# The last 1024 tokens of a first mixture as two tiles of 512, with three sets of inputs

## The chip, the cores and the metric

The program runs on one core of a Trainium2 chip. The metric is the device time of one execution in microseconds (us), lower is better; several executions are timed, and the median is given. The engines are named as in the profile: PE is the tensor engine's matmul stream and PEld its weight loads, DVE the vector engine, ACT the scalar engine, POOL GpSimd, SP the engine that issues the DMAs here.

## The reference, cut to what matters

All arrays are float32; the batch is 4, with 8 heads, 576 positions and 64 features.

```python
def attn(q, k, v):                       # (4, 8, 576, 64) each
    # pooled: means over 4 neighbours, full softmax attention over 144 positions, repeated 4 times
    out_up = np.repeat(softmax_attn(pool4(q), pool4(k), pool4(v)), 4, axis=2)
    # local: softmax over |i - j| < 4 only
    out_local = banded_softmax(q @ k.T / 8) @ v
    return out_up + out_local

x = attn(q, k, v).transpose(0, 2, 1, 3).reshape(2304, 512)
h = x @ w_in                             # (512, 2048)
x = (h * np.cos(h)) @ w_out              # first mixture
xn = x / np.sqrt(np.mean(x * x, -1, keepdims=True) + 1e-6) * rms_g
g = xn @ w_gate                          # (512, 1536)
out = (g / (1 + np.exp(-g)) * (xn @ w_val)) @ w_out2     # second mixture
```

## The kernel before

**Tokens and tiles.** The 2304 tokens are nine tiles of 256 (`TT`). A batch of the attention has 576 rows, so it covers two tiles and a quarter. Each tile's attention output is split into a high and a low part (`XH`, `XLO`, the tiles `xh` and `xl`), and every product of a mixture is three matmuls: weight high by x high, weight high by x low, weight low by x high. The weights arrive as 64-bit words and are turned into high and low parts on the chip (`w_conv`, L275: a shift on DVE at L287, an ACT step at L291, a merge on DVE at L293, ACT at L295, a subtraction on POOL or DVE at L298). A converted piece occupies one place of 4 KB a partition and stays; a raw piece occupies one for a time. There are 34 places (`NS`), and 8 more (`NX`) once the attention's memory is closed.

**First mixture.** 72 units, eight to a tile (`unit`, L917, and `second`, L976). A unit computes two 128-column chunks of h for 256 tokens, 24 matmuls 256 wide at L935 into one PSUM bank; then kk, t, sin and t again (L951 to L958) on ACT and DVE, and g split into gh and gl (L969, L971). `second` does 24 more matmuls, 256 wide, at L997, which add up in two banks y over the eight units of the tile. `y_out` (L1005) copies the two banks out on ACT (L1011) and stores them to DRAM (`ysc`). `SEQ` mixes the units of tiles 0 and 1; from tile 2 on they follow one another.

**Inputs of a tile.** There are two sets of x (`xt`). A tile's set is released when its last h product is done (L940), and only then can the attention write the tile after next. `block` (L589) is one local attention block of up to 116 rows: transposes (L603), scores (L640, L646), softmax on DVE and ACT, transposes (L680), values (L705), the sum with the pooled output (L715), and xh on ACT and xl on POOL (L727, L729), which wait for the set. Two tokens `blk` bound how many blocks of batches 1 to 3 are under way. `pooled` (L479) is the pooled attention of a head pair; a block waits for its batch's four (`od`).

**Banks.** PSUM has eight banks. During tiles 0 and 1 four are for y, two for h (`hb`), two for the attention (`att`); after tile 0 both h and the attention get one more.

**Second mixture.** `second_mixture` (L1024) starts when the last tile's x is complete and the last first-mixture weight is converted: it closes the attention's memory, adds `NX` places, and loads and converts 36 pieces. These also need the places of first-mixture weights, which are given back as the last tile uses them (L937 to L938, L999 to L1000). `prep` (L1053) loads a tile's y, normalizes it and writes xh and xl (L1095, L1097). `out_unit` (L1121) and `out_second` (L1181) then do 12 chunks for tile 0 alone, 256 wide, and for four pairs of tiles, 512 wide (L1144, L1201).

**Order.** `Order` writes out the instruction order of all engines ahead of time. Each part (a unit, a block, a conversion) is a generator that yields an engine with an assumed duration, waits for an event or takes a token; the part that can start first goes next, and among nearly equal ones the one with the earlier due time (`DU`, `due`). The assumed durations shape only the order; on the chip, semaphores decide.

Of the kernel before, what the change touches and what calls it, by code (L numbers as in the profile page):

```python
# [25 lines left out]
NX = 42 - NS  # L26
# [3 lines left out]
NQK, NV = 4, 3  # L30
# [14 lines left out]
DU = {"conv": 20, "pool": -260, "blk": -150}  # L45


class Order:
# [65 lines left out]
    def start(self, p):  # L114
# [60 lines left out]
def fused_kernel(ctx: ExitStack, tc, q, k, v, w_in, w_out, w_gate, w_val, w_out2, rms_g, mask, bmask, out):  # L175
# [18 lines left out]
    for n, c in (("t", 2), ("kk", 2), ("g", 2), ("xt", 2), ("n1", 2), ("sq", 1), ("raw", NRAW), ("cv", NCV),  # L194
                 ("blk", 2), ("blk0", 2), ("b2", 5), ("rq", NQK), ("vb", NV), ("od", 2), ("E", 2), ("qs", NQS), ("vh", 2)):
        S_.pool(n, range(c))
# [111 lines left out]
    XH, XLO = (xr.tile([128, 2, 4, TT], F32R, tag=n, name=n) for n in ("xh", "xl"))  # L308
# [81 lines left out]
    def pq_load(b, parts):  # L390
        for w, c, x, m in parts:
            p = yield take("pq")
            t = ap.tile([128, 576], F32, tag=p, name="pq")[:, :512].rearrange("p (u r d) -> p u r d", u=2, r=4)
# [38 lines left out]
    EP = [ap.tile([72, 2, 3, 2, 64], F32, tag=f"E{x}", name="E") for x in range(2)]  # L432
# [13 lines left out]
    def pv(b, hp, t=None, place=None, vh=None):  # L446
# [4 lines left out]
        else:  # L451
# [3 lines left out]
            for _ in range(2):  # L455
                x = yield take("pq")
                p.append(x)
            t = (ap.tile([128, 576], F32, tag=p[0], name="v4")[:, :512].rearrange("p (c x) -> p c x", c=2),
                 ap.tile([128, 576], F32, tag=p[1], name="v4")[:, :256])
# [129 lines left out]
    def block(b, u, raw, pools):  # L589
# [5 lines left out]
        yield take(tok)  # L595
        T = []
# [51 lines left out]
        for x, _ in T:  # L648
            give("b2", x)
        t0 = (S_.cur["t"], "PE")  # L650
# [136 lines left out]
    def start():  # L787
# [3 lines left out]
        for n in [("pq", w, c) for c in range(3) for w in range(2)] + [("qs", w) for w in range(2)] + [("E", hp) for hp in (2, 3)] \  # L791
# [17 lines left out]
        E = EP + [early(("E", hp), [72, 2, 3, 2, 64]) for hp in (2, 3)]  # L809
# [3 lines left out]
        for hp in range(2):  # L813
            yield take("E")
# [57 lines left out]
        S_.add(after(("od", 0), "E", 0, 1), 0.0)  # L872
        S_.add(after(("od", 0), "pq", "pq1"), 0.0)
        S_.add(after(("od", 0), "place", pl["E", 2], pl["E", 3]), 0.0)
# [27 lines left out]
    G = {}  # L902

    def moe():
# [10 lines left out]
        + [(t, u) for t in range(2, NTILE) for u in range(8)]  # L915

    def unit(n):  # L917
        t, u = SEQ[n]
        yield wait(("x", t))
        xh, xl, xi = X[t]  # L920
        for ci in range(2):
            yield wait(("w", 1, 2 * (2 * u + ci)))
# [4 lines left out]
        h3 = bank_tile(i, [128, 2, TT], "h")  # L927
        for ci in range(2):
            wh, wl = W[1, 2 * (2 * u + ci)]
            yield "PE", 1.44  # L930
# [10 lines left out]
        h = h3.rearrange("p c t -> p (c t)")  # L941
# [23 lines left out]
        gh = tp.tile([128, 2, TT], F32R, tag=f"gh{g_i}", name="gh")  # L965
        gl = tp.tile([128, 2, TT], F32R, tag=f"gl{g_i}", name="gl")
        tv = t.rearrange("p (c t) -> p c t", c=2)
        yield "ACT", 0.62
        ACT.activation(out=gh, in_=tv, func=ACTF.Copy)  # L969
        _, e = yield [("POOL", 1.5), ("DVE", 0.8, None, None, GLB)]  # L970
        (POOL if e == "POOL" else DVE).tensor_tensor(out=gl, in0=tv, in1=gh, op=ALU.subtract)  # L971
# [4 lines left out]
    def second():  # L976
        y, yi = {}, {}
        for n in range(8 * NTILE):
            t, u = SEQ[n]
            S_.due(T0 + U1 * n + DS)  # L980
            yield wait(("g", n))
            for ci in range(2):
                yield wait(("w", 1, 2 * (2 * u + ci) + 1))
            if u == 0:
                yi[t] = []
                for _ in range(2):
# [292 lines left out]
```

## Time and profile before

| | us |
|---|---|
| median of 3 executions | 1057.72 (1054.84 to 1058.4) |
| the profiled execution | 1062.11 |
| its span, first to last instruction | 1060.3 |
| PE busy in the span | 1019.4 (96%) |
| DVE / ACT / POOL busy | 518.6 / 491.0 / 252.8 |
| mean granted TensorE clock | 0.982 of full speed |

The span and the rows below are of the profiled execution, which took 4.4 us more than the median. A busy share of a long stretch hides stages with different limits, so the stages are read one by one.

### The profile page before, as it was taken

Reading aid. Unit: us, or ns where it says so; the run is one execution under the profiler, and the core shown is the slowest. Engines: PE = TensorE matmul, PEld = TensorE weight load, DVE = VectorE, ACT = ScalarE, POOL = GpSimd, SP = SyncE. Lnnn points to the kernel's source line nnn. Section 1 sums busy time; section 2 is a strip of 40 time slices with the busy share of each in tenths; the row PEclk is TensorE's granted clock in tenths of the full one; section 3 lists DMA queues with packets and bytes.
Section 4 is the critical chain, followed back from the end, with each engine's and each line's share of the span. In section 5 each row is a group of like instructions: output and inputs, shape, how many; then the busy total and the mean of one; then the engine's idle time right before and its main releaser. Section 6 shows DMA issues by size and latency. Waiting matters only on the chain.

```text
span 1060.3 us, 18859 instructions
## 1 busy us (share of the span) xinstructions
PE 1019.4 (96%) x7736; PEld 927.9 (88%) x7736; DVE 518.6 (49%) x866; ACT 491.0 (46%) x897; POOL 252.8 (24%) x303
## 2 busy tenths in 40 slices
PE   7888889999999999999999988999999999999998
PEld 7788789999999999999999976888888888888886
DVE  3688964655564545344488887312341153112112
ACT  4656785675675445363567865311331142122111
POOL 3857674345441000000044443000000000000000
PEclk9889989999999999999999999999999999999999
DMA  8769532443331111100436550100200020001001
GB/s 237 204 179 280 178 90 77 115 120 95 98 79 29 46 33 49 38 22 2 160 115 224 168 190 2 39 1 1 70 11 1 1 80 1 0 1 40 1 1 40
DMA packets 108134, 82.57 MB, mean 78 GB/s; under 512 B 67344, under 2 KB 95120, under 8 KB 108048
## 3 DMA queue, kind: packets, MB, share of 16 engines
q1 hardware_dynamic: 108048, 81.36, 25.9%
q8 instruction: 61, 1.00, 0.4%
q14 instruction: 25, 0.20, 0.1%
HBM read 71.90 MB, written 9.44 MB: 77 GB/s over the span
## 4 chain that ended last, share of the span: by engine, by line
PE 84%; DVE 8%; ACT 3%; issue 2%; DMA 1%; SPq 1%; POOL 0%; ACTq 0%; DVEq 0%; POOLq 0%
PE gvp L1144 25%; PE y L997 18%; PE h L935 17%; PE o L1201 13%; DVE raww L293 2%; PE bav L705 2%; PE btr L603 2%; PE warm L226 1%; DVE raww L287 1%; PE avp L553 1%; PE bs L646 1%; PE bat L680 1%; ACT E L509 1%; DMA raww<-in_moe_w_in 1%; PE sps L498 1%
## 5 line engine op out<-in xcount | busy, mean ns | idle before, releaser
L1144 PE MATMUL gvp<-xh,ww 128*128 128x512 f32 (+1 forms) x840 | 245.1, 370 | 0.0
L935 PE MATMUL h<-xh,ww 128*128 128x256 f32 x1152 | 225.6, 289 | 4.0 <-DVE t L958 4.0
L997 PE MATMUL y<-gh,ww 128*128 128x256 f32 x1152 | 225.1, 289 | 0.6 <-ACT gh L969 0.6
L935 PEld LDWEIGHTS h<-xh,ww 128*128 128x128 f32 x1152 | 186.7, 194 | 5.9 <-DVE t L958 2.9
L997 PEld LDWEIGHTS y<-gh,ww 128*128 128x128 f32 x1152 | 185.5, 193 | 2.8 <-ACT gh L969 1.1
L1144 PEld LDWEIGHTS gvp<-xh,ww 128*128 128x128 f32 x840 | 154.0, 190 | 26.4
L997 PE MATMUL y<-gl,ww 128*128 128x256 f32 x576 | 164.2, 285 | 4.1 <-DVE gl L971 4.1
L935 PE MATMUL h<-xl,ww 128*128 128x256 f32 x576 | 164.2, 285 | 0.0
L1164 DVE TENSOR_TENSOR sil<-gvp,sil 128x512 f32<-128x512 f32 (+1 forms) x60 | 38.2, 637 | 257.3 <-PE gvp L1144 249.4
L1144 PE MATMUL gvp<-xl,ww 128*128 128x512 f32 (+1 forms) x420 | 155.2, 370 | 0.0
L997 PEld LDWEIGHTS y<-gl,ww 128*128 128x128 f32 x576 | 111.0, 193 | 5.1 <-DVE gl L971 5.1
L935 PEld LDWEIGHTS h<-xl,ww 128*128 128x128 f32 x576 | 111.6, 194 | 0.0
L1159 ACT ACTIVATE sil<-gvp 128x512 f32<-128x512 f32 (+1 forms) x60 | 33.2, 553 | 156.9 <-PE gvp L1144 156.8
L298 POOL TENSOR_TENSOR ww<-raww,ww 128x512 fp32r<-128x512 f32 x56 | 81.6, 1467 | 56.0 <-ACT ww L295 43.3
L1174 ACT ACTIVATE uh<-sil 128x512 fp32r<-128x512 f32 (+1 forms) x60 | 35.2, 587 | 124.8 <-DVE sil L1164 124.4
L1144 PEld LDWEIGHTS gvp<-xl,ww 128*128 128x128 f32 x420 | 79.7, 190 | 13.3
L953 DVE SCALAR_TENSOR_TENSOR t<-kk,h 128x512 f32<-128x512 int32 x72 | 49.0, 681 | 79.7 <-ACT kk L951 79.4
L1201 PE MATMUL o<-ww,uh 128*128 128x512 f32 x252 | 78.5, 393 | 0.0
L958 DVE TENSOR_TENSOR t<-h,t 128x512 f32<-128x512 f32 x72 | 48.8, 687 | 33.6 <-ACT t L956 33.4
L951 ACT ACTIVATE kk<-h 128x512 int32<-128x512 f32 x72 | 42.5, 591 | 48.1 <-PE h L935 47.6
L729 POOL TENSOR_TENSOR xl<-bt,xh 128x464 fp32r<-128x464 f32 (+16 forms) x28 | 25.9, 931 | 149.0 <-ACT xh L727 148.7
L1201 PE MATMUL o<-wx,uh 128*128 128x512 f32 x180 | 56.5, 396 | 2.5 <-ACT uh L1174 2.5
(134 smaller groups left out, 1592.3 us busy)
## 6 DMA issues: line engine op xcount, KB each, us to landing
raww<-in_moe_w_out SPq DMA_DIRECT2D x25, 512.0 KB, 5.3
raww<-in_moe_w_in SPq DMA_DIRECT2D x16, 512.0 KB, 5.3
vb<-in_v SPq DMA_DIRECT2D x80, 64.0 KB, 2.6
raww<-in_moe_w_gate SPq DMA_DIRECT2D x10, 512.0 KB, 5.0
ysc<-yst SPq DMA_DIRECT2D x18, 256.0 KB, 2.4
y<-ysc SPq DMA_DIRECT2D x9, 512.0 KB, 3.9
raww<-in_moe_w_val SPq DMA_DIRECT2D x9, 512.0 KB, 5.3
out<-ost SPq DMA_DIRECT2D x18, 256.0 KB, 2.0
```

What stands on the lines that cost most here:

```text
L298: (POOL if e == "POOL" else DVE).tensor_tensor(out=w[:, 1], in0=c, in1=w[:, 0], op=ALU.subtract)
L729: POOL.tensor_tensor(out=xl, in0=bx[:, :, at:at + l], in1=xh, op=ALU.subtract)
L935: PE.matmul(h3[:, ci, :], a[:, ksl], x[:, kk, :], start=m == 0, stop=m == 11)
L951: ACT.activation(out=kk, in_=h, func=ACTF.Copy, scale=INV2PI, bias=0.25)
L953: DVE.scalar_tensor_tensor(out=t, in0=kk, scalar=TWOPI, in1=h, op0=ALU.mult, op1=ALU.subtract)
L958: DVE.tensor_tensor(out=t, in0=h, in1=t, op=ALU.mult)
L997: PE.matmul(y[t][f // 2][:, f % 2, :], a[:, fsl], g[:, ci, :], start=(u == 0 and ci == 0 and i == 0 and f % 2 == 0), stop=(u == 7 and ci = ...
L1144: PE.matmul(g, a[:, ksl], x[:, kk, :] if w_ == 1 else x[:, :, kk, :], start=m == 0, stop=m == 11)
L1159: ACT.activation(out=sl, in_=gate, func=ACTF.Silu)
L1164: DVE.tensor_tensor(out=sl, in0=g, in1=sl, op=ALU.mult)
L1174: ACT.activation(out=uh[:, :n_], in_=sl, func=ACTF.Copy)
L1201: PE.matmul(o[m], a[:, msl], w, start=(c == 0 and i == 0), stop=(c == 11 and i == 2))
```

## The change

The first mixture's tiles 5 to 8 become two double tiles of 512 tokens, (5, 6) and (7, 8). A unit of these computes one 128-column chunk of h for 512 tokens, in 12 matmuls 512 wide, and the second product 12 more; 16 units make a double tile. The count of units stays 72, and so do the shapes of the elementwise steps (128x512). The output of a double tile takes four banks, and its `y_out` copies them alternately on ACT and DVE, with two DMAs each.

There are three sets of x instead of two. For their memory `NX` falls from 8 to 6, the raw q and k tiles of blocks from four to two (`NQK`), the buffers E of the pooled attention from two to one (three instead of two then lie in weight places for batch 0), and the `pq` tiles from 576 to 512 elements. There are three `blk` tokens instead of two, with a token `T` for the scores stage. The banks: h keeps two until the end; the attention has two, then four after tile 0, and two again from the first output of tile (5, 6). The due times of the pooled attention and of the blocks are 60 and 50 us earlier, and the planner takes a bank for the attention later, by the slack that it assumes.

```diff
-NX = 42 - NS
+NX = 40 - NS
-NQK, NV = 4, 3
+NQK, NV = 2, 3
-DU = {"conv": 20, "pool": -260, "blk": -150}
+DU = {"conv": 20, "pool": -320, "blk": -200}
...
-            return max(p["t"], min(have, key=lambda x: x[0])[0]), None
+            t = p["t"]
+            if r[1] == "att" and p["slack"] and p["eng"] not in ("PE", "?", None):
+                t += p["slack"] + self.LAT
+            return max(t, min(have, key=lambda x: x[0])[0]), None
...
-("xt", 2), ... ("blk", 2), ("blk0", 2), ... ("E", 2)
+("xt", 3), ... ("blk", 3), ("T", 1), ("blk0", 2), ... ("E", 1)
...
-    XH, XLO = (xr.tile([128, 2, 4, TT], F32R, tag=n, name=n) for n in ("xh", "xl"))
+    XH, XLO = (xr.tile([128, 3, 4, TT], F32R, tag=n, name=n) for n in ("xh", "xl"))
...
+    T1S = [(0,), (1,), (2,), (3,), (4,), (5, 6), (7, 8)]
...
-        + [(t, u) for t in range(2, NTILE) for u in range(8)]
+        + [(j, u) for j in range(2, len(T1S)) for u in range(8 * len(T1S[j]))]
+    def chunks(n):
+        j, u = SEQ[n]
+        c = (2 * u, 2 * u + 1) if len(T1S[j]) == 1 else (u,)
+        return j, c, u == 0, c[-1] == 15
+    def xs(ts, o=0):
+        ts = sorted(ts, key=lambda t: X[o + t][2])
+        i = [X[o + t][2] for t in ts]
+        if len(ts) == 1:
+            return XH[:, i[0]], XLO[:, i[0]], ts
+        return (*(x[:, i[0]:i[1] + 1:i[1] - i[0]] for x in (XH, XLO)), ts)
...
     def unit(n):
-        t, u = SEQ[n]
-        yield wait(("x", t))
+        j, cs, _, last = chunks(n)
+        for t in T1S[j]:
+            yield wait(("x", t))
...
-                    PE.matmul(h3[:, ci, :], a[:, ksl], x[:, kk, :], start=m == 0, stop=m == 11)
+                    PE.matmul(h[:, w_ * ci:w_ * ci + w_], a[:, ksl], x_at(x, kk), start=m == 0, stop=m == 11)
-            if t == NTILE - 1:
-                give("place", WP[1, 2 * (2 * u + ci)])
-        if u == 7:
-            give("xt", xi)
+            if j == len(T1S) - 1:
+                give("place", WP[1, 2 * c])
+        if last:
+            for t in T1S[j]:
+                give("xt", X[t][2])
...
     def second():
+            if first:
+                if len(T1S[j]) == 2 and len(T1S[j - 1]) == 1:
+                    for _ in range(2):
+                        yield take("att")
+                for _ in range(w_ // 128):
                     x = yield take("bank")
...
-                        PE.matmul(y[t][f // 2][:, f % 2, :], a[:, fsl], g[:, ci, :], ...)
+                        PE.matmul(y[j][b][:, k, :], a[:, fsl], g[:, w_ * ci:w_ * ci + w_], ...)
...
     def y_out(j, y, yi):
+            if i % 2 and len(ts) == 2:
+                yield "DVE", 0.7, t0
+                DVE.tensor_copy(out=st, in_=y[i].rearrange("p f t -> p (f t)"))
...
+                    SP.dma_start(ysc[t, :, TT * i:TT * i + TT], st[:, TT * s:TT * s + TT])
...
-        if t == 0 and LK:
-            give("att", 0)
+        if j == 0:
+            for _ in range(2):
+                give("att", 0)
+        if j == len(T1S) - 1:
             give("hb", 0)
```

## Rows read from the trace of the kernel before

**Rows 1.** Windows of five stages: us, busy us of each engine (instructions), clock, DMA

```profile
core 0: us, PE busy (x) PEld busy (x) DVE busy (x) ACT busy (x) POOL busy (x), PEclk, DMA share, GB/s
75.00:175.00 100.00, 88.73 (x750) 85.06 (x749) 76.05 (x118) 71.09 (x142) 69.04 (x76) 0.95 0.58 173
175.00:387.50 212.50, 210.95 (x2247) 204.19 (x2246) 116.12 (x228) 127.51 (x256) 70.97 (x113) 1.00 0.30 78
387.50:590.00 202.50, 202.50 (x1930) 200.51 (x1929) 116.16 (x189) 115.20 (x184) 38.41 (x32) 1.00 0.28 86
590.00:666.00 76.00, 66.87 (x431) 59.35 (x430) 60.73 (x91) 48.35 (x82) 29.33 (x20) 0.96 0.37 120
666.00:1060.30 394.30, 390.57 (x1726) 322.82 (x1724) 103.59 (x156) 88.57 (x130) 0.00 (x0) 1.00 0.05 18
```

**Rows 2.** Chain that ended last, in order of time: start, us, what

```profile
379.06 8.64 PE y L997 x72
...
661.68 2.81 PE gvp L1144 x11
...
665.85 5.45 PE gvp L1144 x24
...
696.04 10.88 PE gvp L1144 x48
```

**Rows 3.** Timeline of PE at tile 5 and at the change of mixtures: start, us

```profile
387.54 0.28 PE L935 MATMUL h<-xh,ww 128*128 128x256 f32 x1
...
590.11 0.28 PE L1144 MATMUL gvp<-xh,wx 128*128 128x256 f32 x1
...
598.47 0.28 PE L1144 MATMUL gvp<-xh,wx 128*128 128x256 f32 x1
```

**Rows 4.** Waits of PE from 585 to 668 us: total, times, longest

```profile
PE o L1201 <- DVE ul L1176: 4.9, 4, 1.7
PE o L1201 <- ACT uh L1174: 2.5, 1, 2.5
```

**Rows 5.** Timeline of DVE: first and last conversion

```profile
530.78 0.42 DVE L287 TENSOR_SCALAR raww<-raww 128x512 int32<-128x512 int32 x1
...
643.62 1.81 DVE L293 SCALAR_TENSOR_TENSOR raww<-raww 128x512 int32<-128x512 int32 x1
```

**Rows 6.** Windows around the conversion of the second mixture's weights

```profile
497.00:531.00 34.00, 34.00 (x333) 33.61 (x332) 16.85 (x29) 17.82 (x28) 2.45 (x2) 1.00 0.41 136
531.00:645.00 114.00, 108.43 (x834) 104.27 (x833) 100.03 (x147) 85.54 (x140) 51.24 (x37) 0.99 0.49 159
```

**Rows 7.** Timeline of POOL: the low part of x

```profile
424.21 0.79 POOL L729 TENSOR_TENSOR xl<-bt,xh 128x256 fp32r<-128x256 f32 x1 [12.94 <-ACT xh L727]
...
525.56 1.15 POOL L729 TENSOR_TENSOR xl<-bt,xh 128x448 fp32r<-128x448 f32 x1 [16.76 <-ACT xh L727]
```

**Rows 8.** Timeline of ACT: x written, pooled output ready [idle before, releaser]

```profile
335.92 0.29 ACT L561 ACTIVATE od<-avp 128x144 f32<-128x144 f32 x1 [4.50 <-PE avp L553]
337.35 1.03 ACT L727 ACTIVATE xh<-bt 128x416 fp32r<-128x416 f32 x2 [1.13 <-PE h L935]
...
390.62 0.94 ACT L727 ACTIVATE xh<-bt 128x320 fp32r<-128x320 f32 x2 [8.00 <-PE h L935]
...
423.72 0.42 ACT L727 ACTIVATE xh<-bt 128x256 fp32r<-128x256 f32 x1 [1.22 <-DVE bt L715]
...
494.27 0.78 ACT L727 ACTIVATE xh<-bt 128x112 fp32r<-128x112 f32 x2 [0.80 <-PE h L935]
```

**Rows 9.** Timeline of ACT around a unit's h, and a prep's xh

```profile
572.75 0.60 ACT L951 ACTIVATE kk<-h 128x512 int32<-128x512 f32 x1 [1.72 <-PE h L935]
...
659.32 1.05 ACT L1095 ACTIVATE xh<-y 128x1024 fp32r<-128x1024 f32 x1
```

**Rows 10.** Timeline of DVE: the step that frees that unit's bank of h

```profile
575.43 0.69 DVE L958 TENSOR_TENSOR t<-h,t 128x512 f32<-128x512 f32 x1 [0.79 <-ACT t L956]
```

**Rows 11.** Groups of instructions: count | busy us, mean ns | idle before

```profile
L661 DVE TENSOR_REDUCE bst<-bt 128x8 f32<-128x512 f32 x15 | 10.2, 679 | 3.7 <-ACT bt L659 3.7
```

More of the change, by code (lines that the diff above doesn't have):

```diff
@@ L429, in fused_kernel @@
     vd = {}
-    EP = [ap.tile([72, 2, 3, 2, 64], F32, tag=f"E{x}", name="E") for x in range(2)]
+    EP = [ap.tile([72, 2, 3, 2, 64], F32, tag=f"E{x}", name="E") for x in range(1)]
     VH = [ap.tile([128, 3, 128], F32, tag=f"vh{x}", name="vh") for x in range(2)]
@@ L595, in block @@
         yield take(tok)
+        if b:
+            yield take("T")
         T = []
@@ L812, in start @@
             POOL.memset(E[hp], 0.0)
-        for hp in range(2):
-            yield take("E")
+        yield take("E")
         for hp in range(4):
@@ L926, in unit @@
         done(("h", n), 0.0)
[L927 to L930, printed above, removed]
+        w_ = 512 // len(cs)
+        h = bank_tile(i, [128, 512], "h")
+        for ci, c in enumerate(cs):
+            wh, wl = W[1, 2 * c]
+            yield "PE", 1.44 if len(cs) > 1 else 2.76
             m = 0
@@ L964, in unit @@
         done(("go", n), 0.0)
-        gh = tp.tile([128, 2, TT], F32R, tag=f"gh{g_i}", name="gh")
-        gl = tp.tile([128, 2, TT], F32R, tag=f"gl{g_i}", name="gl")
-        tv = t.rearrange("p (c t) -> p c t", c=2)
+        gh = tp.tile([128, 512], F32R, tag=f"gh{g_i}", name="gh")
+        gl = tp.tile([128, 512], F32R, tag=f"gl{g_i}", name="gl")
         yield "ACT", 0.62
-        ACT.activation(out=gh, in_=tv, func=ACTF.Copy)
+        ACT.activation(out=gh, in_=t, func=ACTF.Copy)
         _, e = yield [("POOL", 1.5), ("DVE", 0.8, None, None, GLB)]
-        (POOL if e == "POOL" else DVE).tensor_tensor(out=gl, in0=tv, in1=gh, op=ALU.subtract)
+        (POOL if e == "POOL" else DVE).tensor_tensor(out=gl, in0=t, in1=gh, op=ALU.subtract)
         give("t", t_i)
@@ L978, in second @@
         for n in range(8 * NTILE):
-            t, u = SEQ[n]
+            j, cs, first, last = chunks(n)
             S_.due(T0 + U1 * n + DS)
             yield wait(("g", n))
[L982 to L986, printed above, removed]
+            for c in cs:
+                yield wait(("w", 1, 2 * c + 1))
+            w_ = 512 // len(cs)
+            if first:
+                if len(T1S[j]) == 2 and len(T1S[j - 1]) == 1:
+                    for _ in range(2):
+                        yield take("att")
+                yi[j] = []
+                for _ in range(w_ // 128):
@@ L994, in second @@
                 for f in range(4):
                     fsl = slice(f * 128, f * 128 + 128)
+                    b, k = divmod(f, 512 // w_)
                     for i, (a, g) in enumerate(((wh, gh), (wh, gl), (wl, gh))):
-                        PE.matmul(y[t][f // 2][:, f % 2, :], a[:, fsl], g[:, ci, :], start=(u == 0 and ci == 0 and i == 0 and f % 2 == 0),
-                                  stop=(u == 7 and ci == 1 and i == 2), skip_group_check=True)
-                if t == NTILE - 1:
-                    give("place", WP[1, 2 * (2 * u + ci) + 1])
+                        PE.matmul(y[j][b][:, k, :], a[:, fsl], g[:, w_ * ci:w_ * ci + w_], start=(first and ci == 0 and i == 0 and k == 0),
+                                  stop=(last and c == 15 and i == 2), skip_group_check=True)
@@ L1001, in second, with y_out @@
+                if j == len(T1S) - 1:
+                    give("place", WP[1, 2 * c + 1])
             give("g", g_i)
-            if u == 7:
-                S_.add(y_out(t, y[t], yi[t]), T0 + U1 * (n - 2))
-    def y_out(t, y, yi):
-        for i in range(2):
-            tag = ("t", "kk")[i]
+            if last:
+                S_.add(y_out(j, y[j], yi[j]), T0 + U1 * (n - 2))
+    def y_out(j, y, yi):
+        ts = xs(T1S[j])[2]
+        t0 = (S_.cur["t"], "PE")
+        for i in range(len(yi)):
+            tag = ("t", "kk")[i % 2]
@@ L1027, in second_mixture @@
         attn_ctx.close()
-        for _ in range(2):
-            yield take("att")
+        yield take("att")
         P2["wx"] = ctx.enter_context(tc.tile_pool(name="wx", bufs=1, reuse_waits="tile"))
@@ L1183, in out_second @@
             j, c = divmod(n, 12)
-            rows = [TT * t + 128 * m for t in sorted(T2[j], key=lambda t: X[100 + t][2] if len(T2[j]) == 2 else 0) for m in range(2)]
             S_.due(due2(n))
@@ L1188, in out_second @@
             yield wait(("w", 2, 3 * c + 2))
+            rows = [TT * t + 128 * m for t in xs(T2[j], 100)[2] for m in range(2)]
             if c == 0:
```

62 lines of the change are left out of this document (33 added, 29 removed).

## Prediction

> **What bounds the kernel now.** Stages first, because a share of the whole span would mix five different limits. In the windows by stage [rows 1], PE is busy without a gap from 387.5 to 590 us, where tiles 5 to 8 of the first mixture run, at the full granted clock; nearly so from 175 to 387.5, and again from 666 on. In these three stages only fewer or shorter matmuls can help. Two stages differ. From 75 to 175 us PE is idle for 11 of 100 us, with DVE, ACT and POOL all between 69 and 76 us busy: the first weights are converted there. From 590 to 666 us, the change from one mixture to the other, PE is busy for 66.9 of 76 us at a granted clock of 0.96, while DVE is busy for 60.7.
>
> Next the chain of waits, for the price of a matmul [rows 2]. Undisturbed runs of 256-wide ones give 8.64 us for 72, or 120.0 ns each; the 512-wide ones of the second mixture give 10.88 us for 48, or 226.7 ns each. Both are streams with a new weight load for every matmul, both with the same three products.
>
> For the change of mixtures I take the timeline of PE [rows 3] and the waits [rows 4]. The first mixture's last products end with the 598.47 row; the first pair's gate product starts in earnest at 661.68 and the chain goes on from 665.85 without a break [rows 2]. Tile 0 of the second mixture is 12 chunks of 24 matmuls at 120.0 and 6 at 226.7 ns, so 12 x 4.24 = 50.9 us; 1.44 of it ran early, from 590.11, and 2.72 of the next pair ran before 665.85. So 52.2 us of matmuls took 67.4: 15.2 us are lost. The waits name DVE (ul 4.9) and ACT (uh 2.5), half of it; the rest is the lower clock and small gaps. Both steps queue among the conversions of the second mixture's weights: the first is at 530.78 us and the last starts at 643.62 [rows 5], and in between DVE is busy for 100.0 of 114 us [rows 6].
>
> **The change part by part.**
>
> *Wide matmuls.* 32 units (tiles 5 to 8) trade 48 matmuls of 120.0 ns for 24 of 226.7: 5.76 against 5.44 us, so 32 x 0.32 = 10.2 us, in a stage where PE is the bound. The x operand becomes two strided parts, as it already is in the pairs whose 226.7 ns I use; sets that aren't neighbours only change the stride. The elementwise steps keep shape and count.
>
> The rows give 13.3 ns saved for each pair of 256-wide matmuls. The Trainium skill ("TensorE: Matmul & The Clock Gate", "Back-to-back issue gap") gives 262 cycles for 256 columns and 518 for 512 at 2.4 GHz, so merging two saves only 6 cycles; by that the term would be an estimated 1.9 us (768 pairs x 2.5 ns), and most of the case for width would be gone.
>
> *When the pairs can start.* Tile (5, 6) needs x of tile 6 at its first unit, 387.5 us in the old trace [rows 3]. Before, it came at 425.0 [rows 7], because its set was released by tile 4 at 390.6 [rows 8]. Now the third tile back releases it: tile 3, at 337.4. The pooled output of batch 3, which its last block needs, was there at 336.2. After the release at 390.6 that block, which had waited for a token, took 33 us to 423.7, so it would end near 371 even if it only started at 337.4; the third token lets it start sooner. I put no stall here, with 16 us in hand.
>
> Tile (7, 8) needs x of tile 8, whose set comes free with the last product of tile (5, 6). That is 16 units in, so 16 x 0.32 = 5 us before the old 494.3, near 489. Before, only two blocks waited there and the last one, without a token, finished at 526.7 [rows 7]; with three tokens, all three can wait with their sums done, and then write: on ACT 0.8 for two and some 0.5 for the third (1.03 for two at 337.4), with POOL behind it (1.15 for a large one), so about 4 us. PE has one or two second products of 2.72 us in hand, so I charge 2 us (bounds 0 and 4, the latter if no second product is left).
>
> *The change of mixtures.* The second mixture's loads wait for x of tile 8. It comes at 493 instead of 526.7; with the same 4.1 us to the first conversion, 497 instead of 530.8. From 497 to 531 DVE was busy for only 16.9 of 34 us [rows 6]. The work of DVE from 497 to 645, 16.9 + 100.0 = 116.9 us, at the share of the later window (100.0/114 = 0.877) takes 133 us: the conversions end at 630 instead of 645. The weight places allow it: they come free two a unit from unit 56 on, where four a unit came from unit 64. With the old tail behind the last conversion, the pairs go on at 651 instead of 665.9, 15 us sooner. This includes the 10.2 us of the wide matmuls and isn't added to them: the later of two chains counts. The other is PE's own: 665.9 - 10.2 - 15.2 = 640.4, plus 2 at the boundary, 642. Bounds: 0 from the conversions (DVE fills no idle time, and the loss stays 15.2; the gain is then the 10.2 less the boundary) and 25 (PE's own chain).
>
> *Third set in the second mixture.* Tile 2's xh was written at 659.3 [rows 9], after tile 0's last product released a set; now its set is free when the first mixture ends. That takes up to 2 us off the tail; the three later pair boundaries had little to give (390.6 busy of 394.3 us from 666 on). I take 1 us together (bounds 0 and 3).
>
> *Edits that I cost at nothing.* Two banks of h: the unit whose h is read at 572.75 [rows 9] frees its bank at 576.1 [rows 10], 3.4 us, and PE has a second product and the other bank's first to do, 5.4 us; with only one product of 2.72 as cover, 0.7 us a unit would show. The four copies of y go half to ACT and half to DVE, both below 60% busy there, during the next product. The double tiles' eight output DMAs in place of four lie on SP's queue where the DMA share is 0.28; behind them wait the weight loads, with 5 raw buffers. Six places in place of eight matter only if the conversion ran ahead of the returned ones. The wait of `second` for two `att` tokens holds the y product of unit 40 in the written order; behind it on PE are only later products, and h of unit 41 can go first.
>
> *The front.* One buffer E serializes the pooled attention, and earlier blocks bring their DVE and ACT steps into the stage from 75 to 175, where these are at 70 to 76%. Against that, PE has 11 us idle there to take their matmuls. I take 0 (bounds: 8 lost, two blocks of six DVE steps in the scores stage at no more than the 0.68 of the largest [rows 11]; 11 gained, all the idle time).
>
> **Sum.** Profiled execution 1062.1, less 15 and less 1: 1046. The median lies 4.4 below the profiled one, so 1057.7 - 16 = 1042.
>
> **Rivals.**
>
> *Conversions don't fill the gap* (1047 to 1054): the units' steps go ahead in the order, or ACT, which each piece needs twice, holds DVE up, and only the wide matmuls count: 10.2, less 0 to 6 at the boundaries and the front. For it: ACT is busy for 85.5 of the 114 us itself; against it: half of DVE is free from 497 to 531.
>
> *PE's chain decides* (1031 to 1037): everything lost at the change of mixtures comes back. Against it: DVE would have to be busy for more than 0.877, or the tail of 21 us behind the last conversion be 9 us shorter.
>
> *The other side, x of tile 6 late* (1061 to 1085): if the attention doesn't run a tile further ahead, because one E and two raw tiles slow it, the double tile waits for x and each us late is a us lost. With the old 425.0 that is 37 us. It turns the sign once x of tile 6 comes later than about 403 (387.5 plus the 16 gained). Against it are the 16 us in hand worked out above.
>
> *No difference* (1054.6 to 1060.9): a front that loses what the width gives.
>
> *Width is worth nothing* (1044 to 1051): two 256-wide matmuls would cost no more than one 512-wide. First conversion at 502 then, end at 635, pairs at 656: 10 us from the conversions and 1 from the third set, less 0 to 4 at the boundary. [rows 2] are streams of the very form that comes, which leaves it little. The Trainium skill's table, above, would come near this case, and the trace here disagrees with it.
>
> **How the numbers follow.** Forecast (1037 to 1047) 0.45; conversions don't fill 0.22; PE's chain 0.13; x late 0.10; no difference 0.08; width worth nothing 0.02. The first, second, third and last are faster: 0.82; same 0.08; slower 0.10. About 0.3% is what a measurement of this kernel can tell from no change. The range 1031 to 1055 takes in the forecast, the conversions' rival and PE's chain, and leaves out about 0.18.
>
> **What would show it.** Right: h and y in double tiles at 2.72 us for 12 matmuls; x of tile 6 before the last unit of tile 4; the first second-mixture conversion near 497 and the last near 630; PE on the first pair's unbroken stretch near 651. Wrong: PE idle before unit 40 with ACT's xh as the releaser; a longer idle stretch before 175; or conversions that start earlier and still end near 645.

## The result and the profile after

The changed kernel takes 1042.68 us (median of 4 runs, 1040.64 to 1047.96) against 1056.99 for the kernel before beside it: ratio 0.989, 95% interval 0.9863 to 0.9916. The profiled execution takes 1043.55 us with a span of 1041.8. Forecast were 1042 and, for the profiled one, 1046. The time came out. The gain did less so: forecast were 15.7 us, measured are 14.3 here and 9.7 when both kernels ran again side by side (1054.94 and 1045.28), and the forecast ratio, 0.985, lies just below both 95% intervals. One of the steps behind the number did not come out at all.

Windows by stage of the changed kernel, cut at its own first 512-wide h product and its own last y product, in the columns of [rows 1]:

```profile
core 0: us, PE busy (x) PEld busy (x) DVE busy (x) ACT busy (x) POOL busy (x), PEclk, DMA share, GB/s
75.00:175.00 100.00, 90.04 (x802) 86.19 (x801) 80.39 (x131) 78.90 (x139) 70.75 (x76) 0.93 0.57 163
175.00:393.70 218.70, 217.99 (x2406) 210.15 (x2405) 121.99 (x245) 143.87 (x284) 78.37 (x122) 1.00 0.32 83
393.70:589.50 195.80, 190.52 (x974) 156.50 (x973) 133.73 (x195) 114.56 (x183) 52.62 (x39) 0.99 0.35 111
589.50:645.00 55.50, 53.05 (x369) 48.67 (x368) 36.15 (x61) 32.17 (x53) 9.39 (x7) 1.00 0.19 58
645.00:1041.80 396.80, 393.02 (x1739) 325.17 (x1737) 102.53 (x156) 87.33 (x129) 0.00 (x0) 1.00 0.05 18
```

In [rows 1] the stage of tiles 5 to 8 had no idle PE and the stage behind it had 9 us. Now it is the other way round: 5.3 us idle in the first, 2.5 in the second. The chain of waits prices the new products (start, us, what):

```profile
436.69 8.38 PE y L1027 x36
445.07 8.16 PE h L961 x36
...
643.65 2.72 PE gvp L1179 x12
647.73 2.73 PE gvp L1179 x12
```

36 matmuls in 8.16 us are 226.7 ns each, the price taken from [rows 2]. The last two rows stand against 661.68 and 665.85 there: behind tile 0 of the second mixture the pairs go on at 647.7. The waits of PE from 560 to 645 us (total, times, longest) stand against [rows 4], and the timeline of PE shows where the three of y are:

```profile
PE y L1027 <- ACT gh L994: 2.4, 1, 2.4
PE o L1236 <- DVE ul L1211: 1.9, 3, 1.0
PE y L1027 <- DVE gl L996: 1.7, 1, 1.7
PE y L1027 <- POOL gl L996: 0.7, 1, 0.7
PE o L1236 <- ACT uh L1209: 0.5, 1, 0.5
```

```profile
575.50 0.50 PE L1027 MATMUL y<-gl,ww 128*128 128x512 f32 x1 [0.73 <-POOL gl L996]
...
580.72 0.50 PE L1027 MATMUL y<-gh,ww 128*128 128x512 f32 x1 [2.42 <-ACT gh L994]
...
582.90 0.79 PE L1027 MATMUL y<-gl,ww 128*128 128x512 f32 x1 [1.69 <-DVE gl L996]
```

What was lost on the second mixture's ul and uh (7.4 us in [rows 4], now 2.4) is in good part lost on the first mixture's gh and gl (4.8 us). The view of [rows 4] has one row of y, not shown there:

```profile
PE y L997 <- DVE gl L971: 0.7, 2, 0.5
```

All three waits of y in the changed kernel lie behind its last h product, at 571.4 us, where no h product is left to fill the time. The timeline of DVE just before shows what the last units' steps (L979, L984, L996) stand among:

```profile
572.84 3.23 DVE L290 TENSOR_SCALAR raww<-raww 128x512 int32<-128x512 int32 x3
575.99 1.21 DVE L1138 TENSOR_TENSOR xl<-y,xh 128x1024 fp32r<-128x1024 f32 x1
577.12 0.68 DVE L979 SCALAR_TENSOR_TENSOR t<-kk,h 128x512 f32<-128x512 int32 x1
577.72 0.68 DVE L1110 TENSOR_TENSOR sq<-sq 128x512 f32<-128x512 f32 x1
578.32 0.68 DVE L296 SCALAR_TENSOR_TENSOR raww<-raww 128x512 int32<-128x512 int32 x1
578.92 0.68 DVE L984 TENSOR_TENSOR t<-h,t 128x512 f32<-128x512 f32 x1
...
580.46 1.79 DVE L296 SCALAR_TENSOR_TENSOR raww<-raww 128x512 int32<-128x512 int32 x1
582.17 0.68 DVE L996 TENSOR_TENSOR gl<-t,gh 128x512 fp32r<-128x512 f32 x1
```

L290 and L296 are the second mixture's conversions, L1110 and L1138 its preparation of x: work for later, ahead of work for which PE waits. The conversions begin where [rows 5] had 530.78 and end where it had 643.62, by the timeline of DVE:

```profile
495.97 0.42 DVE L290 TENSOR_SCALAR raww<-raww 128x512 int32<-128x512 int32 x1
...
607.16 1.29 DVE L296 SCALAR_TENSOR_TENSOR raww<-raww 128x512 int32<-128x512 int32 x2
```

The timeline of ACT answers [rows 8]: the pooled output of batch 3, x of tile 6, x of tile 8.

```profile
372.95 0.29 ACT L564 ACTIVATE od<-avp 128x144 f32<-128x144 f32 x1
...
376.79 0.42 ACT L734 ACTIVATE xh<-bt 128x256 fp32r<-128x256 f32 x1 [1.10 <-DVE bt L722]
...
488.63 1.25 ACT L734 ACTIVATE xh<-bt 128x112 fp32r<-128x112 f32 x3 [1.97 <-PE h L961]
```

**The account used below.** For each run I took PE's matmuls from the timeline, start to start. "A" is the time beyond 120.0 or 226.7 ns a matmul from unit 56's first h product to the last y product (76 short matmuls of the attention, which lie there in `before`, `before_again` and `one_E`, are left out with their own 2.75 us); "B" is the same from there to the first 512-wide gate product of the second mixture, that is of the first pair; "from 16" is the time from unit 16's first h product to the end of the last matmul, which leaves out the front. "Conversions" gives the start of the first and of the last DVE step of the second mixture's conversions. A difference in the front tells nothing here: two profiles of the kernel before reach unit 16 at 211.5 and 204.1 us, the changed kernel at 207.6 and 210.5.

```
run          A     B   from 16   conversions     median us   ratio (95%)
before      1.7  13.2   845.2   530.8 to 643.6   1056.99     -
before_again 1.8 11.2   843.1   523.4 to 635.8   1056.49   0.9996 (0.9974-1.0018)
after       8.4   3.7   830.3   496.0 to 607.8   1042.68   0.9890 (0.9863-0.9916)
after_again 9.9   3.8   832.2   499.1 to 612.4   1045.28   0.9905 (0.9879-0.9932)
singles     5.7   5.2   840.6   454.2 to 633.2   1053.74   0.9982 (0.9961-1.0004)
late_loads  7.3   7.2   833.1   524.8 to 637.7   1045.59   0.9904 (0.9875-0.9933)
hb3        12.2   3.8   838.5   497.4 to 612.4   1052.28   0.9966 (0.9941-0.9990)
two_sets    9.1   5.3   834.3   501.5 to 614.0   1048.81   0.9926 (0.9897-0.9954)
last_pair   0.1   3.0   827.6   451.4 to 597.4   1039.29   0.9846 (0.9818-0.9875)
real_dur    3.7   3.7   825.8   491.3 to 604.8   1039.35   0.9838 (0.9810-0.9866)
pair_dur    0.3   0.1   824.6   454.5 to 599.2   1038.91   0.9844 (0.9824-0.9865)
conv_back   8.8   2.7   829.9   498.7 to 610.2   1040.76   0.9867 (0.9843-0.9891)
loads_after 7.8  43.5   869.8   561.7 to 675.1   1078.14   one run
one_E       4.7  11.1   849.6   526.1 to 638.5   1058.55   1.0033 (1.0015-1.0051)
```

From unit 16 on the change is worth 845.2 - 830.3 = 14.9 us by the first profiles, 10.9 to 14.9 over the four pairs of them; 0.9 us of it are short matmuls of the attention that the change puts ahead of unit 16 (1119 in place of 1142 behind it). The ratios are each to the kernel before as it ran beside that run; `before_again`, `two_sets`, `last_pair` and `real_dur` ran on another chip than the rest of the experiments, without the changed kernel beside them, and the kernel before alone differs by up to 2 us between the groups of runs (1054.94 to 1056.99), so their distance from the changed kernel is no better known than that. A + B went from 14.9 (13.0) to 12.1 (13.7): little came back at the change of mixtures.

### The profile page after: what moved, and what is told of

It reads as the page before. It is cut to its first block, busy times and chain, and to the rows that moved or that the text cites. A ratio compares the mean times of both kernels' runs of the same rounds, so it can differ in the third digit from the quotient of the medians.

```text
span 1041.8 us, 17345 instructions
## 1 busy us (share of the span) xinstructions
PE 1005.4 (97%) x6968; PEld 883.7 (85%) x6968; DVE 519.6 (50%) x876; ACT 498.6 (48%) x895; POOL 258.0 (25%) x305
## 4 chain that ended last, share of the span: by engine, by line
PE 77%; DVE 11%; issue 4%; SPq 3%; ACT 2%; DMA 2%; POOL 1%; DVEq 0%; ACTq 0%; POOLq 0%
PE gvp L1179 27%; PE y L1027 14%; PE h L961 14%; PE o L1236 14%; DVE raww L296 3%; DVE raww L290 2%; PE bav L712 2%; PE btr L608 1%; DMA raww<-in_moe_w_in 1%; PE avp L556 1%; DVE t L979 1%; PE bs L651 1%; DVE gl L996 1%; SPq L442 1%; DVE t L984 1%
## 5 line engine op out<-in xcount | busy, mean ns | idle before, releaser
L1027 PE MATMUL y<-gh,ww 128*128 128x256 f32 (+1 forms) x896 | 212.4, 320 | 4.1 <-ACT gh L994 4.1
L961 PE MATMUL h<-xh,ww 128*128 128x256 f32 (+1 forms) x896 | 212.6, 320 | 2.1 <-DVE t L984 2.1
L1027 PEld LDWEIGHTS y<-gh,ww 128*128 128x128 f32 x896 | 152.7, 192 | 16.3 <-ACT gh L994 5.0
L961 PEld LDWEIGHTS h<-xh,ww 128*128 128x128 f32 x896 | 152.6, 192 | 13.6 <-DVE t L984 2.5
L1027 PE MATMUL y<-gl,ww 128*128 128x256 f32 (+1 forms) x448 | 142.2, 317 | 3.9 <-DVE gl L996 3.0
L961 PE MATMUL h<-xl,ww 128*128 128x256 f32 (+1 forms) x448 | 141.1, 315 | 0.3 <-POOL xl L736 0.3
L1236 PE MATMUL o<-ww,uh 128*128 128x512 f32 x360 | 111.1, 390 | 0.5 <-ACT uh L1209 0.5
L961 PEld LDWEIGHTS h<-xl,ww 128*128 128x128 f32 x448 | 86.1, 192 | 5.6 <-POOL xl L736 0.7
L979 DVE SCALAR_TENSOR_TENSOR t<-kk,h 128x512 f32<-128x512 int32 x72 | 49.0, 680 | 62.3 <-ACT kk L977 62.1
L1236 PEld LDWEIGHTS o<-ww,uh 128*128 128x128 f32 x360 | 67.1, 188 | 14.1 <-ACT uh L1209 0.7
L1236 PE MATMUL o<-ww,ul 128*128 128x512 f32 x180 | 70.4, 391 | 1.9 <-DVE ul L1211 1.9
L984 DVE TENSOR_TENSOR t<-h,t 128x512 f32<-128x512 f32 x72 | 49.2, 686 | 29.1 <-ACT t L982 28.8
```

Source lines behind the costliest of these rows:

```text
L961: PE.matmul(h[:, w_ * ci:w_ * ci + w_], a[:, ksl], x_at(x, kk), start=m == 0, stop=m == 11)
L979: DVE.scalar_tensor_tensor(out=t, in0=kk, scalar=TWOPI, in1=h, op0=ALU.mult, op1=ALU.subtract)
L984: DVE.tensor_tensor(out=t, in0=h, in1=t, op=ALU.mult)
L1027: PE.matmul(y[j][b][:, k, :], a[:, fsl], g[:, w_ * ci:w_ * ci + w_], start=(first and ci == 0 and i == 0 and k == 0), stop=(last and c == ...
L1236: PE.matmul(o[m], a[:, msl], w, start=(c == 0 and i == 0), stop=(c == 11 and i == 2))
```

## The experiments

The theory of the prediction: the pairs start when the conversions are through, and earlier x of tile 8 brings both forward. Its rival: PE's own stream sets the pairs' start, the conversions are needed nowhere as early as they come, and the gain is the width's.

**The same two kernels again** (after_again, before_again). 

> The changed kernel once more, as the mark for the others of this call. All theories: 1041 to 1044 us, 13 to 16 us under the kernel before.

> The kernel before once more, for a second profile of it. Theory (the loss at the change of mixtures belongs to its order of work): between the last y product and the first product of the first pair some 13 us beyond the matmuls again, and the last conversion near 644. Rival (the first profile, 5 us over the median, was unlucky just there): under 8 us.

Measured 1045.28 and 1056.49. The second profile of the kernel before loses 11.2 us in B and ends its conversions at 635.8, so the loss was not the first profile's bad luck; the 7.4 us by which its front is shorter is what two profiles of one program can differ by.

**No double tiles** (singles).

```diff
-    T1S = [(0,), (1,), (2,), (3,), (4,), (5, 6), (7, 8)]
+    T1S = [(t,) for t in range(NTILE)]
```

> The changed kernel with nine single tiles of 256 in the first mixture, all else kept (three sets of x, banks, buffers, due times). Theory (width on PE, and weight places that come free over the last 16 units, so that the second mixture's weights are converted earlier): the 10.2 us of the width are lost; x of tile 8 is there early, but only 8 places are free until the last eight units, so the last conversion ends near 630 to 645 and 4 to 8 us of the change of mixtures come back on top: 1054 to 1060 us. Rival (three sets and the attention run ahead give the gain): 1041 to 1046. Rival (width alone): 1051 to 1054, with the last conversion still near 608.

Measured 1053.74, ratio 0.9982 (0.9961 to 1.0004): the time of "width alone", with the last conversion at 633, as the first theory had it. Beside the changed kernel of the same chip the width is worth 8.5 us by medians and, from unit 16 on, 840.6 - 831.3 (the mean of the two profiles) = 9.3 us by the traces, of 10.2 forecast. The rest of the change is worth 1 us by the median (its interval also takes in no gain) and 3.6 us from unit 16 on (844.2, the mean of the two profiles before, less 840.6). That rest includes conversions that began at 454.2, 77 us sooner than in [rows 5]: the first sign that their start isn't worth its time. And y waits on gl here too, without any double tile (waits of PE from 495 to 603 us, the longer of the two rows):

```profile
PE y L1027 <- DVE gl L996: 3.3, 3, 1.5
```

**Conversions as late as before** (late_loads). The second mixture's loads also wait for unit 62:

```diff
     def second_mixture():
         yield wait(("x", NTILE - 1))
+        yield wait(("h", 62))
```

> The changed kernel, but the second mixture's weight loads and preparation wait in the written order until h of unit 62 is under way, near 526 us, where they began in the kernel before; the width is untouched. Theory (half of the gain is the earlier start of the conversions): first conversion near 528 to 531, last near 635 to 645, the loss at the change of mixtures back by 8 to 12 us: 1050 to 1055. Rival (the gain is the width, and the conversions would have fitted anyway): 1041 to 1045.

Measured 1045.59 against 1045.28 with the early ones. The conversions run from 524.8 to 637.7, within 7 us of [rows 5], and the gain is still there. Windows of DVE before and in its conversions:

```profile
497.00:525.00 28.00, 28.00 (x126) 23.17 (x125) 13.79 (x22) 12.74 (x21) 0.00 (x0) 1.00 0.62 209
525.00:639.00 114.00, 105.60 (x563) 89.25 (x562) 108.12 (x154) 84.91 (x140) 58.16 (x37) 0.99 0.49 157
```

The last conversion is 25 to 30 us later than in the two profiles of the changed kernel, and the pairs go on behind tile 0 at 651.9 us against 647.7 and 652.3 there. The theory of the prediction falls: from the last conversion's end to that point it had 21 us, and there are 39 in the changed kernel and 13.5 here. B is 3.4 us above the changed kernel's, A 1.1 to 2.6 below.

The waits of PE from 493 to 590 us show something that the theory of early conversions doesn't explain:

```profile
PE y L1027 <- ACT gh L994: 2.0, 1, 2.0
PE y L1027 <- DVE gl L996: 1.6, 2, 0.9
...
PE y L1027 <- POOL gl L996: 0.3, 1, 0.3
```

The conversions are as late as in the kernel before, and y still waits 3.9 us on gh and gl, where the kernel before waits 0.7.

**A third bank for h in the last double tile's time** (hb3).

```diff
-        if j == len(T1S) - 1:
-            give("hb", 0)
...
         yield take("att")
+        give("hb", 0)
```

(the first in `y_out`, the second in `second_mixture`)

> The changed kernel with a third bank for h from the start of the second mixture's loads on, near 490 us, where it now comes only at the end of the first mixture. Theory of the prediction (two banks of h cost nothing, the PE idle time of 4.9 us from 575 to 592 is the late gh and gl behind the conversions on ACT and DVE): within 2 us of the changed kernel. Rival (h runs out of banks, and with a third the last units run ahead): 3 to 7 us faster, 1036 to 1040, with no PE idle time there.

Measured 1052.28, 7 us slower than the changed kernel. The longest of the waits of PE from 454 to 602 us:

```profile
PE y L1027 <- DVE gl L996: 6.5, 8, 1.8
```

With a bank more, h runs further ahead: in units 56 to 61 the y product starts 14 to 21 us behind the unit's last h product, in the changed kernel 8.4 to 8.8. Even so gl is late eight times. Two banks of h are not what the last units lack. Why a bank more costs 7 us isn't shown beyond these waits.

**Two sets of x in the second mixture** (two_sets).

```diff
-            for t in T1S[j]:
+            for t in T1S[j][:1 if j == len(T1S) - 1 else 2]:
                 give("xt", ...)
```

> The changed kernel with one set of x withheld after the last double tile, so that the second mixture has two sets as before; the first mixture is untouched. Since a later start of the conversions changed nothing, theory A is that the third set, which lets the inputs of tiles 1 and 2 be prepared without waiting for tile 0, is what shortened the change of mixtures: 4 to 8 us slower than the changed kernel, 1049 to 1053, with PE waiting for xl before the first pair. Theory B (the width is nearly all of the gain): 1 to 3 us slower.

Measured 1048.81, just under theory A's range. The timeline of PE shows the wait that the third set takes away:

```profile
651.32 0.50 PE L1179 MATMUL gvp<-xh,wx 128*128 128x512 f32 x1 [1.48 <-ACT xh L1136]
652.58 0.50 PE L1179 MATMUL gvp<-xl,wx 128*128 128x512 f32 x1 [0.76 <-DVE xl L1138]
```

It is worth 2.2 us in these two rows and 2 to 4 us from unit 16 on, where 1 was forecast (bounds 0 and 3).

**Only tiles 7 and 8 as a double tile** (last_pair).

```diff
-    T1S = [(0,), (1,), (2,), (3,), (4,), (5, 6), (7, 8)]
+    T1S = [(0,), (1,), (2,), (3,), (4,), (5,), (6,), (7, 8)]
```

> The changed kernel with only tiles 7 and 8 in a double tile; 5 and 6 are single. Theory (10.2 us of width for 32 units, 8.5 measured by the singles): 16 units less of it, 4 to 5 us slower, 1049 to 1050. Rival (the boundary between the double tiles, where x of tile 8 is written after the release, costs some us, and it is gone here): 1044 to 1047. Rival (the four banks of y and the late gh and gl at the end are what counts): as the changed kernel or slower than 1052.

Measured 1039.29, ratio 0.9846, below what all three expected: half the width (5.1 us of matmuls more) and yet faster. Tile 8's x now waits for a set that a single tile frees, and is written from 444 in place of 489 us on; the conversions spread over 146 us in place of 112, and A falls to 0.1. The spread alone can't be the reason: in the run without double tiles they spread over 179 us, and A is 5.7.

**True durations in the written order** (real_dur). The order is written with assumed durations; for the second mixture's two DVE steps of a conversion they become 0.75 and 0.9 us in place of 0.34 and 0.70, near the mean that the profile shows (0.77 and 0.93 for L290 and L296 in the changed kernel, groups from 491 to 608 us):

```profile
L296 DVE SCALAR_TENSOR_TENSOR raww<-raww 128x512 int32<-128x512 int32 x30 | 27.3, 927 | 1.6 <-ACT raww L294 1.4
L290 DVE TENSOR_SCALAR raww<-raww 128x512 int32<-128x512 int32 x30 | 22.2, 766 | 0.0
```

```diff
-        a = yield "DVE", 0.34
+        a = yield "DVE", (0.34, 0.75)[m - 1]
...
-        yield "DVE", 0.7
+        yield "DVE", (0.7, 0.9)[m - 1]
```

> The changed kernel with the planner's assumed DVE durations of the second mixture's conversions raised from 0.34 and 0.70 to 0.75 and 0.90 us, near what the trace shows (0.78 and 0.93); only the written order changes. Theory (the 8 us lost at the end of the first mixture are units' gh and gl behind more conversions than the order counted on): 2 to 6 us faster, 1039 to 1043, with less PE waiting on gh and gl from 575 to 592. Rival (the order is as good as it gets, the two engines are simply full): within 2 us, or slower.

Measured 1039.35, 3 to 6 us below the changed kernel: A is 3.7 in place of 8.4 and 9.9. More than the order changed. The order also picks DVE or POOL for each gl by the durations that it assumes, and it gave POOL 15 of the 72 gl in place of 11 (8 in place of 4 from 430 us on). Which of the two did it, no run separates.

**Both together** (pair_dur).

> Only tiles 7 and 8 as a double tile, and the order written with DVE durations of 0.75 and 0.9 us for the second mixture's conversions. Theory A (the loss before the last y product comes from conversion steps that stand ahead of the last units' steps in the written order; with early conversions or true durations it is gone): both edits take away the same loss, so they don't add up. Up to the last y product 0 to 1 us of idle PE as with the one double tile alone, 3 to 4 us after it, time 1036 to 1041, that is 0 to 3 us below the one double tile alone (1039.3). Theory B (each edit removes a loss of its own): the 3 to 6 us that the durations gave the changed kernel come off once more, 1033 to 1036. Conversions still end before 610 us in both.

Measured 1038.91 (1038.22 to 1039.27). The wait on gl and gh was one loss, and the two edits don't add up by the median; from unit 16 on the traces differ by 3.0 us, nearly all of it idle time (A + B 3.1 and 0.4; theory A had 3 to 4 us left behind the last y product, and 0.1 is left). The order gave POOL 22 of the 72 gl here and 11 in the run with the one double tile alone. The waits of PE from 451 to 645 us have one row left:

```profile
PE y L1027 <- POOL gl L996: 1.0, 1, 1.0
```

This is the fastest version by the median, 0.4 us ahead of the single edits, which is no difference that a measurement here can tell.

**Conversions ranked behind** (conv_back). (In the expectations "theory A" and "theory B" are other things than A and B of the account.)

```diff
-        return T0 + T1 * NTILE + (i // 3) * U2 + (0.0, 0.0, 4.0)[i % 3] + DU["conv"]
+        return T0 + T1 * NTILE + (i // 3) * U2 + (0.0, 0.0, 4.0)[i % 3] + DU["conv"] + 400
```

> The changed kernel with the second mixture's conversions due 400 us later, so that the written order puts a unit's own steps ahead of them wherever both are ready. Theory A (rank and assumed duration of the conversions in the written order starve the last units): the idle PE before the last y product falls from 8.4 to between 1 and 5 us, conversions end later, at 610 to 640 us, and 4 to 10 us are lost after the last y product; time 1040 to 1047. Theory B (the order's rank has no part, the steps are late because the engines as such are full): 7 to 10 us before the last y product as in the changed kernel, last conversion near 608, time 1041 to 1046.

Measured 1040.76 (1038.45 to 1045.64), A 8.8. Theory A asked for 1 to 5 and for conversions that end at 610 to 640; they ended at 610.2. So the later due time hardly moved them: 64 of their 72 DVE steps lie between unit 56's first h product and the last y product, 63 in the changed kernel. The run shows that this due time has little say, not what an order with the conversions behind the units would give. The waits of PE from 494 to 646 us, and the timeline of DVE ahead of the longest:

```profile
PE y L1027 <- DVE gl L996: 4.4, 3, 2.1
...
PE y L1027 <- ACT gh L994: 0.3, 1, 0.3
```

```profile
574.44 2.37 DVE L1131 SCALAR_TENSOR_TENSOR y<-y,cst,rs 128x256 f32<-128x256 f32 x2
576.73 0.68 DVE L996 TENSOR_TENSOR gl<-t,gh 128x512 fp32r<-128x512 f32 x1
```

Here a step of the second mixture's preparation (L1131) stands ahead of gl and takes 2.37 us for two.

**Fewer conversions beside the last units** (loads_after).

```diff
     def second_mixture():
         yield wait(("x", NTILE - 1))
+        yield wait(("h", 71))
```

> The changed kernel whose second mixture's weights are loaded only after the first mixture's last h product. Theory A (conversions starve the last units): with no conversion beside them the idle PE between unit 56 and the last y product is 0 to 3 us in place of 8.4, and the whole bill comes after it: first conversion near 590, last near 690, 35 to 60 us idle there, time 1075 to 1100. Theory B (double tiles by themselves starve, by their two banks of h): 6 to 9 us are still lost before the last y product.

Measured 1078.14 in its one run. The waits of PE from 486 to 680 us, those ahead of the last y product being the last three shown:

```profile
PE o L1237 <- ACT uh L1210: 7.1, 5, 3.2
PE gvp L1180 <- POOL ww L301: 6.5, 5, 1.9
...
PE gvp L1180 <- ACT xh L1137: 3.1, 1, 3.1
...
PE gvp L1180 <- DVE xl L1139: 1.1, 1, 1.1
PE h L961 <- POOL xl L736: 0.3, 1, 0.3
```

The row of y with gh or gl is gone, as theory A has it. The sum that it gave for A is not (7.8 where 0 to 3 were expected): a gate product of tile 0 now stands ahead of the last y products in PE's order and waits for x of the second mixture. That wait, at 577 us, falls into the stretch in which the changed kernel's y waited, and the conversions began at 561.7 and not near 590, so 17 of their DVE steps still lie beside the last units. The run agrees with theory A but doesn't prove it. The bill behind the last y product, 43.5 us, is in the expected 35 to 60.

**One buffer E alone, in the kernel before** (one_E). E's pool, its releases and its tokens go from two to one:

```diff
-    EP = [ap.tile([72, 2, 3, 2, 64], F32, tag=f"E{x}", name="E") for x in range(2)]
+    EP = [ap.tile([72, 2, 3, 2, 64], F32, tag=f"E{x}", name="E") for x in range(1)]
```

> The kernel before with one buffer E. By the prediction's account of the front (E serializes the pooled attention, its cost hidden): time within 3 us of the kernel before, 1053 to 1060. By what the changed kernel's trace shows (pooled output of batch 3 ready at 373 in place of 336 us) the same must show here: its last pooled step at 355 to 375, and x of tile 6 and everything behind it unchanged to 3 us, since in this order x of tile 6 waits for its set until 390. The other theory, that two raw tiles and not E are what makes the pooled attention late: it stays near 336.

Measured 1058.55, ratio 1.0033 (1.0015 to 1.0051). Its timeline of ACT shows the pooled output of batch 3:

```profile
369.97 0.29 ACT L561 ACTIVATE od<-avp 128x144 f32<-128x144 f32 x1 [1.51 <-PE avp L553]
```

So one E explains the 336 to 373 of the changed kernel, and alone it costs 1.6 to 5.4 us by the interval. Its account shows how far an edit of the attention reaches: with 44 conversion steps beside the last units, where the kernel before has 43, y waits 3.1 us on gl, and there 0.7. (Its "from 16" also holds 2.6 us more of the attention's matmuls than the kernel before's.)

## Why the prediction was right, and where not

*Wide matmuls: right.* 226.7 ns in the stream, 10.2 us forecast, 9.3 in the traces from unit 16 on, 8.5 in the medians. The rival "width is worth nothing" falls. The Trainium skill's table for an isolated matmul ("TensorE: Matmul & The Clock Gate", "Back-to-back issue gap") would have the term at an estimated 1.9 us; the traces here disagree.

*When the pairs can start: right in what it gives, wrong in one row.* x of tile 6 was written at 376.8, first used at 393.8: 17 us in hand, 16 forecast. But the pooled output was not "there at 336.2"; one E brought it at 372.95, 4 us ahead of its use. The step took a row of the kernel before for an event that another part of the change moves, and got away with it. At tile 8 all three blocks wrote together as forecast (488.63, three in 1.25 us); PE waited 0.3 us where 2 were charged.

*The change of mixtures: this step failed.* The first conversion came at 496.0 (497 forecast), so loads, places and x of tile 8 were read rightly. The last came at 607.8, not 630. Two terms were off: from 497 to then DVE was busy for 104.0 of 110.8 us, 0.94 where 0.877 was assumed, and 13 of the 116.9 us of work in the sum did not have to be done by then. The rival "conversions don't fill the gap" falls, with DVE busy for 32.50 of 34 us from 497 to 531 against 16.85 in [rows 6]:

```profile
497.00:531.00 34.00, 33.93 (x150) 27.79 (x149) 32.50 (x46) 26.41 (x45) 17.87 (x12) 1.00 0.71 228
```

The pairs went on at 647.7, between the 651 of the conversions' chain and the 642 of "PE's own chain". Counted from unit 16, that is 14.2 us sooner than in the kernel before by the first profiles (10.3 to 14.2 over the four pairs), so the 15 nearly came out. But not for the reason given. "The later of two chains counts" took the conversions to be what the pairs wait for, and late_loads shows that they weren't: 29 us later at the start, the time stays. Nor did the loss come back, as "PE's own chain" would have it: 4.8 of the 15 us were to come from here beside the 10.2 of the width, and A + B gave 2.8 by the first profiles and -0.7 to 2.8 over all pairs. What left B turned up in A, as waits of y on gh and gl. That the number held is in part luck.

*What makes the last units wait.* Shown: it is gh and gl of the last units (waits), and a third bank of h doesn't mend it (hb3). Not shown: that the conversions, because they come earlier, are the cause. Of their 72 DVE steps this many lie between unit 56's first h product and the last y product, and PE's waits on gh and gl in that stretch are:

```
run          steps   waits of y on gh and gl, us
before         43       0.7
singles        39       4.3
late_loads     43       3.9
last_pair      54       none
pair_dur       54       none
real_dur       59       2.2
after          63       4.8
conv_back      64       4.7
hb3            68       6.5
```

Fewer steps beside the last units don't go with shorter waits. Every edit also writes a new order for all engines, and the places that the last units' steps happen to get in it are a rival that no run here rules out, for the gains of last_pair and real_dur too. How much is the engines' load, how much the place of each step and how much the engine that gl is given to stays open.

*Third set: right in kind, small.* 1 forecast, 2 to 4 measured (two_sets); 1.5 of the wait that it takes away lies in B, so this and the line above overlap.

*Edits at nothing.* In the double tiles PE's h products waited for nothing but x of tile 8, so two banks of h cost nothing there. One E is not nothing by itself (1.6 to 5.4 us); inside the change it can't be told from the rest, which without the width nets 1 us by the median.

*The sum.* 10.2 was 9.3; 4.8 was about 1; the third set's 1 was 2 to 4. The errors nearly cancel, and the forecast of 1042 owes its closeness to that as well as to the width. So the width is the part of the gain whose cause is shown.

## What to carry to other kernels

Price a wider matmul from two streams of the same kernel and multiply: that term held. When a change lets background work start sooner, don't ask only when it ends, but beside whose steps it now runs: a loss that leaves one side of a boundary may appear on the other. Count the wait in several orders before you name its cause: here runs with the same number of conversion steps beside the last units waited 0.7 and 3.9 us. Where an order is written with assumed durations, put in the measured ones and look whether work has changed its engine too; here the two together gave 3 to 6 us, and 0.4 by the median once only tiles 7 and 8 were a double tile.

## What the hardware showed unasked

The DVE conversions have two durations. In the changed kernel's second mixture all 20 of L290 and all 21 of L296 that ran with no POOL instruction beside them took 0.41 to 0.42 and 0.68 to 0.69 us. The 16 and 15 others, which overlap one, took up to 1.55 and 1.81 (means 1.20 and 1.24), some 21 us of DVE more than at the short values. In the fence of DVE above, L296 takes 0.68 at 578.32 and 1.79 at 580.46; the timeline of POOL has its next instruction at 580.22:

```profile
580.22 1.48 POOL L301 TENSOR_TENSOR ww<-raww,ww 128x512 fp32r<-128x512 f32 x1 [4.77 <-ACT ww L298]
```

The order of the starts tells the two values apart. All 23 lengthened steps began behind the start of a POOL instruction that still ran, and each ended a fixed time after that instruction's end: 0.28 to 0.29 us for L290 and 0.55 us for L296. The 8 that kept the short value in spite of an overlap began before the POOL instruction or, one of them, together with it. So what a lengthened step adds is the rest of the POOL instruction, less 0.13 us. The Trainium skill ("SBUF — State Buffer", "SBUF: two separate sides") says that DVE and GpSimd share one pair of ports, which one instruction holds to its end while the other waits; the rows agree. The assumed 0.34 us lies below even the short value; 0.70 is the short value, and what it misses is the time behind POOL.

PE's clock also answered: behind the idle stretches the changed kernel's next matmuls ran at the lower of the two levels, 0.50 being 1.2 GHz, and then at the full one. Windows of 578 to 580.7, 583 to 585.6 and 586 to 589 us:

```profile
578.00:580.70 2.70, 0.29 (x2) 0.00 (x0) 2.70 (x6) 2.70 (x6) 0.48 (x1) 1.00 0.87 295
583.00:585.60 2.60, 2.60 (x6) 2.05 (x7) 2.60 (x5) 1.11 (x2) 1.30 (x1) 0.50 0.55 182
586.00:589.00 3.00, 3.00 (x15) 2.48 (x14) 3.00 (x6) 1.46 (x3) 1.22 (x1) 1.00 0.40 142
```

Six matmuls in 2.6 us where eleven fit at 226.7 ns: some 1.2 us of A is the clock's and not the wait's. In the second profile the same two waits were followed by 14 matmuls in 5.8 us, from 586.6 to 592.4, where 3.2 would do, at a granted clock of 0.53 from 586 to 592.5: 2.6 of its 9.9 us.
